# Gated FFN on one core: constant start-up matmuls in bfloat16 instead of fp8, and the weights of contraction blocks 2 and 3 in four DMAs instead of two

## Chip, cores, metric

One core of a Trainium2 chip. The metric is the device time of one execution in microseconds (us). The profile's span, from the first to the last instruction, is about 1.8 us shorter than the device time of the same execution.

## The reference

```python
def reference(x, w_gate, w_up, w_down):          # gelu with the tanh approximation
    return (_gelu(x @ w_gate) * (x @ w_up)) @ w_down
# x (32, 32, 1024), w_gate and w_up (1024, 3584), w_down (3584, 1024), all bfloat16
```

So 1024 rows, a contraction of 1024 (eight blocks of 128) for gate and up, and one of 3584 for the down projection.

## The kernel before

All instructions of an engine are emitted through one helper, which derives the semaphore waits; the profile therefore gives one line number (L98) to most of it (L163 is a second form of the matmul), and groups are told apart by tile names. `xT` is x transposed, with the contraction on the partitions, `wg` and `wu` are gate and up weights, `ps` is PSUM, `xn` is untransposed x for the first two blocks.

The head of the kernel is what the change touches:

```python
one = nc.const_aps.tensor(1.0, [P, 1], BF16).bitcast(mybir.dt.float8e4)[:, 0:1]
...                                              # identity matrix for the transposes
for n in [512] * 6 + [128] * 2:                  # constant matmuls, result never used
    pr.add("pe", "matmul", ps[:, 3, 0:n], one.broadcast_to([P, 2, P]), one.broadcast_to([P, 2, n]),
           start=True, stop=True, perf_mode=mybir.MatmulPerfMode.DoubleRow, w=[("ps", 3)])

NX = 2
... # x for blocks 0 and 1 (one DMA on each of two queues), then, block by block:
for k in range(NX):
    load_w("sp", "g", 0, k, k + 1)               # 128 KB each
    load_w("act", "u", 0, k, k + 1)
for k0, k1 in ((2, 3), (3, 4), (4, 5), (5, 6), (6, 8)):
    load_x(0, k0, k1)                            # transposing DMAs on SP's queue
load_w("act", "g", 0, 2, 4)                      # 256 KB each, on ACT's queue
load_w("act", "u", 0, 2, 4)
pr.add("act", "activation", warm[:, 0:1], const0, ACTF.Gelu_apprx_tanh)   # loads the table
... # PE transposes of xn for blocks 0 and 1, DVE copies to xT
... # then for k = 0..5: 4 gate matmuls and 4 up matmuls of 512 columns each;
    # after block 0 ACT issues g and u of blocks 4-5, after block 1 those of 6-7
```

In the rest (not shown) TensorE runs through the other weights and the down projection.

## Time and profile before

| | before |
|---|---|
| device time, first three runs | 300.06 us median (299.28 to 300.16) |
| span of the profiled run (299.36 us, not one of the timed runs) | 297.6 us |
| TensorE busy | 294.3 us (99%) |
| first real matmul | 4.76 us |
| first matmul of block 2 | 8.56 us |

First line of the profile page's part 1 (busy us, share of the span, instructions by engine), kernel before. PE are TensorE's matmuls, PEld its weight loads, which overlap them, DVE is VectorE, ACT ScalarE and POOL GpSimd:

```profile
PE 294.3 (99%) x1388; PEld 78.2 (26%) x808; DVE 42.7 (14%) x68; ACT 37.3 (13%) x67; POOL 0.7 (0%) x6
```

TensorE's timeline of the first 10 us, kernel before. The columns are start, duration of the merged group, engine, line, operation, tiles, form and count; in brackets the idle time that the profile shows before it and what ended it:

```profile
0.77 3.01 PE L98 MATMUL ps<-const-bfloat16-1.0 128*128 128x1024 fp8e4 x8 [0.77 <-PEq L310]
3.64 0.92 PE L98 MATMUL ps<-ident,xn 128*128 128x128 bf16 x8
4.76 1.02 PE L98 MATMUL ps<-xT,wg 128*128 128x512 bf16 x4 [0.20 <-DVE xT L98]
5.62 1.03 PE L98 MATMUL ps<-xT,wu 128*128 128x512 bf16 x4
6.49 1.03 PE L98 MATMUL ps<-xT,wg 128*128 128x512 bf16 x4
7.35 1.03 PE L98 MATMUL ps<-xT,wu 128*128 128x512 bf16 x4
8.56 1.02 PE L98 MATMUL ps<-xT,wg 128*128 128x512 bf16 x4 [0.19 <-DMA xT<-in_x_dram]
```

A group of four matmuls at full rate has its successor 0.863 us later (5.62 to 6.49), 0.216 us per matmul. Between 7.35 and 8.56 lie 1.21 us, so TensorE stood still for about 0.35 us; the bracket says 0.19 because the modelled end of a matmul lies behind the moment at which the next one could have started. A group at half rate is longer than 1.03 us: this is how the clock is read here, because the page's clock row shows full clock throughout, also where the spacing is twice as long.

The chain that ended last, kernel before, in order of time (start, us, what); `DMA xT` from 2.21 lasting 6.22 means issued at 2.21 and landed at 8.43:

```profile
2.21 6.22 DMA xT<-in_x_dram
8.43 0.14 issue
8.56 11.60 PE ps L98 x53
```

From 8.56 us on TensorE never waits. In this run the last wait is thus the one for x block 2.

### The profile page before, as it was taken

The numbers are of one execution on the slowest core, as the hardware profiler recorded it, in microseconds if no ns is written. First come the engines' busy times: TensorE is split into PE (matmuls) and PEld (weight loads), VectorE is DVE, ScalarE is ACT, GpSimd is POOL, SyncE is SP. The second block draws the span as 40 slices with busy tenths as digits, with TensorE's granted clock in tenths as the row PEclk, the third lists the DMA queues.
The fourth block names the chain that finished last, engine by engine and source line by source line (L and its number), as shares of the span: only waits on it lengthen the run. The fifth ranks groups of instructions, "written<-read, shape, count | busy, mean of one in ns | idle before, by whom it ended". The sixth has DMA issues, their size and how long they took to land.

```text
span 297.6 us, 2575 instructions
## 1 busy us (share of the span) xinstructions
PE 294.3 (99%) x1388; PEld 78.2 (26%) x808; DVE 42.7 (14%) x68; ACT 37.3 (13%) x67; POOL 0.7 (0%) x6
## 2 busy tenths in 40 slices
PE   8999999999999999999999999999999999999997
PEld 4444322222222222222222222222222222222244
DVE  1030311111221111111111122110000000000000
ACT  1030411111111111221111111110000000000010
POOL 0000000000000000000000000000000000000000
PEclk9999999999999999999999999999999999999999
DMA  7999743006708409321030040000101101011011
GB/s 207 252 241 353 226 134 134 9 0 189 234 2 270 154 2 330 94 76 65 0 139 4 0 141 0 0 2 0 35 0 35 37 0 35 0 37 35 0 35 35
DMA packets 28842, 26.37 MB, mean 89 GB/s; under 512 B 8352, under 2 KB 25248, under 8 KB 28832
## 3 DMA queue, kind: packets, MB, share of 16 engines
q1 hardware_dynamic: 26640, 24.25, 26.3%
q10 hardware_dynamic: 2192, 1.97, 2.2%
q8 instruction: 8, 0.13, 0.2%
q14 instruction: 2, 0.02, 0.0%
HBM read 22.28 MB, written 2.10 MB: 82 GB/s over the span
## 4 chain that ended last, share of the span: by engine, by line
PE 96%; DMA 2%; SPq 0%; issue 0%; ACT 0%
PE ps L98 54%; PE ps L163 42%; DMA xT<-in_x_dram 2%; SPq L98 0%; ACT xT L98 0%
## 5 line engine op out<-in xcount | busy, mean ns | idle before, releaser
L98 PE MATMUL ps<-xT,wg 128*128 128x512 bf16 x256 | 90.2, 379 | 0.4 <-DVE xT L98 0.2
L98 PE MATMUL ps<-xT,wu 128*128 128x512 bf16 x256 | 90.2, 379 | 0.0
L98 PE MATMUL ps<-wd,hT 128*128 128x512 bf16 (+2 forms) x280 | 86.6, 358 | 0.0
L163 PE MATMUL ps<-wd,hT 128*128 128x512 bf16 x196 | 74.3, 379 | 0.0
L163 PE MATMUL ps<-xT,wg 128*128 128x512 bf16 x192 | 72.8, 379 | 0.0
L163 PE MATMUL ps<-xT,wu 128*128 128x512 bf16 x192 | 72.8, 379 | 0.0
L98 DVE TENSOR_TENSOR hT<-g,ps 128x512 bf16<-128x512 f32 x56 | 36.4, 685 | 158.5 <-PE ps L98 158.5
L98 ACT ACTIVATE g<-ps 128x512 f32<-128x512 f32 x56 | 30.8, 595 | 160.4 <-PE ps L98 160.4
L98 PEld LDWEIGHTS ps<-wd,hT 128*128 128x128 bf16 x280 | 26.0, 98 | 71.3 <-issue 65.8
L98 PEld LDWEIGHTS ps<-xT,wu 128*128 128x128 bf16 x256 | 25.0, 98 | 71.7 <-issue 64.1
L98 PEld LDWEIGHTS ps<-xT,wg 128*128 128x128 bf16 x256 | 24.9, 98 | 72.0 <-issue 64.8
L98 DVE CAST xT<-ps 128x512 bf16<-128x512 f32 (+1 forms) x8 | 5.4, 680 | 89.6 <-ACT xT L98 79.8
L98 ACT ACTIVATE xT<-ps 128x512 bf16<-128x512 f32 (+1 forms) x9 | 5.0, 558 | 94.6 <-PE ps L98 94.6
L98 PE MATMUL ps<-const-bfloat16-1.0 128*128 128x1024 fp8e4 (+1 forms) x8 | 3.0, 558 | 0.8 <-PEq L310 0.8
L98 PEld LDWEIGHTS ps<-const-bfloat16-1.0 128*128 128x256 fp8e4 x8 | 1.7, 218 | 1.9 <-issue 1.9
L98 ACT ACT_TABLE_LOAD x1 | 1.3, 1283 | 3.4 <-issue 3.4
L98 DVE COPY xT<-ps 128x256 bf16<-128x256 bf16 x4 | 0.9, 286 | 4.1 <-PE ps L98 4.1
L98 PE MATMUL ps<-ident,xn 128*128 128x128 bf16 x8 | 0.9, 278 | 0.0
L98 PEld LDWEIGHTS ps<-ident,xn 128*128 128x128 bf16 x8 | 0.6, 124 | 0.2
L98 POOL TENSOR_SCALAR_AFFINE_SELECT ident<-ident 128x128 bf16<-128x128 bf16 x1 | 0.3, 292 | 0.2 <-POOL ident L98 0.2
L98 POOL MEMSET ident<- 128x128 bf16 x1 | 0.2, 204 | 0.3 <-POOLq L310 0.3
L98 ACT ACTIVATE warm<-const-float32-0.0 128x1 f32<-128x1 f32 x1 | 0.2, 202 | 0.0
(4 smaller groups left out, 0.4 us busy)
## 6 DMA issues: line engine op xcount, KB each, us to landing
wd<-in_w_down_dram SPq DMA_DIRECT2D x7, 1024.0 KB, 5.4
wg<-in_w_gate_dram SPq DMA_DIRECT2D x6, 1024.0 KB, 7.4
wu<-in_w_up_dram SPq DMA_DIRECT2D x6, 1024.0 KB, 9.7
out_dram<-xT SPq DMA_DIRECT2D x15, 128.0 KB, 1.7
wg<-in_w_gate_dram ACTq DMA_DIRECT2D x3, 256.0 KB, 4.5
wu<-in_w_up_dram ACTq DMA_DIRECT2D x3, 256.0 KB, 4.9
wg<-in_w_gate_dram SPq DMA_DIRECT2D x2, 128.0 KB, 3.2
wu<-in_w_up_dram ACTq DMA_DIRECT2D x2, 128.0 KB, 3.5
```

Of the source, the lines that this page charges most:

```text
L98: ins = name(eng, *args, **kw) if callable(name) else getattr(eng, name)(*args, **kw)
L163: return eng.add_instruction(mybir.InstMatmult(start_tensor_calc=start, stop_tensor_calc=stop, ldweights=False, name=nc.get_next_instructi ...
```

## The change

The likely intent: the constant matmuls keep TensorE occupied so that its clock is up when the real work begins, and are to do that in the number format of the real work; and each weight piece is to arrive in the order of its use, so that block 2 does not wait for weights of block 3.

```diff
-        one = nc.const_aps.tensor(1.0, [P, 1], BF16).bitcast(mybir.dt.float8e4)[:, 0:1]
+        one = nc.const_aps.tensor(1.0, [P, 512], BF16)
 ...
-            pr.add("pe", "matmul", ps[:, 3, 0:n], one.broadcast_to([P, 2, P]), one.broadcast_to([P, 2, n]), start=True, stop=True,
-                   perf_mode=mybir.MatmulPerfMode.DoubleRow, w=[("ps", 3)])
+            pr.add("pe", "matmul", ps[:, 3, 0:n], one[:, 0:P], one[:, 0:n], start=True, stop=True, w=[("ps", 3)])
 ...
-        load_w("act", "g", 0, 2, 4)
-        load_w("act", "u", 0, 2, 4)
+        for k in range(2, 4):
+            load_w("act", "g", 0, k, k + 1)
+            load_w("act", "u", 0, k, k + 1)
```

## The prediction

> **What bounds the kernel now.** TensorE, nearly alone. The busy-share table gives PE 294.3 of a 297.6 us span; the chain that ended last is 96% PE and 2% the DMA that transposes x. In the timeline 512-column matmuls start 0.216 us apart from 8.57 us to the tail without a hole. The work is 1344 of them, about 290 us (estimate from that spacing), so 7.7 us are left, and the change touches only the first 9 us. After its start TensorE waits twice: 0.2 us for the copy of the transposed x and 0.2 us for the DMA of x block 2 (waits view); from the instruction starts the true holes are about 0.2 us at 4.6 and 0.35 us at 8.2.
>
> **Constant matmuls.** Eight run before any data is there, from 0.77 to about 3.6 us. In the timeline the six long ones start 0.427 us apart, twice the later 0.215: half rate, and fp8 with two rows gains nothing. "TensorE: Matmul & The Clock Gate" of the Trainium skill (section "Back-to-back issue gap") gives N/1.2 ns for a cold bf16 matmul, 427 ns at 512. So bf16 should keep 0.427 us each; only the first weight load shrinks (0.18 to 0.1 us), and the block ends perhaps 0.03 us earlier. The transposes behind it wait for the DMAs of x (landed 3.60 and 3.85 us): no gain. Their purpose is to bring the clock up: full-rate spacing appears between 4.2 and 4.4 us, 3.5 us after the first constant matmul, and all real matmuls (from 4.77 us) run at full rate. bf16 keeps TensorE as densely occupied; I expect the same switch. The same page ("What's actually happening") says the window is free-running, so its moment may shift from run to run, worth at most 1.7 us (a 3.4 us window at half rate), for either kernel. The runs before (299.28 to 300.16) may already show this.
>
> **Weights in four pieces.** Same bytes. Two DMA issues of 0.46 and 0.58 us on ScalarE's queue become four, about 1 us more, which moves the activation table load (1.28 us, at 3.37) to about 4.3; the first gelu is at 16.1 us, so this is free. Landings before: g blocks 2-3 at 6.7 us, u at 8.3, x block 2 at 8.43. TensorE needs g and x of block 2 at 8.2 us, u at 9.4, block 3 at 10.3 and 11.2. The last to arrive is x, not a weight. Smaller pieces bring g block 2 to about 6.1 us and u block 2 to about 6.9; both are useless alone. All four pieces are queued before about 5.5 us, so they share the DMA engines with x blocks 2 and 3 much as before; I expect x block 2 at 8.4 +- 0.4 us. Later pieces have over 1.5 us of slack.
>
> **Sum.** Gain at most the 0.35 us hole, expected 0 to 0.1 us; loss under 0.5 us if the transposes come later. Predicted 299.9 us, 8 in 10 between 298.9 and 300.9. Faster by over 2% 0.01, within 2% 0.98, slower by over 2% 0.01.
>
> **What would show it right.** Constant matmuls still 0.427 us apart; real matmuls 0.215 us apart from the first; the wait at 8.3 us still ended by the DMA of x and of like length; PE's busy time the same within 2 us; the u weights of block 2 landing over 1 us earlier with no effect.
>
> **What would make it wrong.** bf16 ones not releasing the clock in time (real matmuls 0.43 us apart until about 7 us, +1 to 2 us), or doing so sooner in most runs (down to -1 us); the regrouped weight DMAs delaying x block 2, which each 0.1 us pays in full.

## The result

| | before | after |
|---|---|---|
| device time, six runs each, median | 300.08 us (299.28 to 300.16) | 299.37 us (298.96 to 299.97) |
| ratio after to before | | 0.9983, 95% interval 0.9968 to 0.9998 |
| span of the profiled run | 297.6 us | 297.9 us |

A ratio is the mean time of one kernel's fast runs over that of the other's of the same rounds, so not quite the ratio of the medians in the table. The timed runs say 0.17% less; the profiled run of after is longer than that of before. The two point in opposite directions, and both are small: this was the first sign that single runs of the same kernel differ by as much as the kernels do.

Part 1 of the page, kernel after:

```profile
PE 294.5 (99%) x1388; PEld 77.9 (26%) x808; DVE 42.7 (14%) x68; ACT 37.3 (13%) x67; POOL 0.7 (0%) x6
```

TensorE's timeline of the first 10 us, kernel after:

```profile
0.77 2.93 PE L98 MATMUL ps<-const-bfloat16-1.0 128*128 128x512 bf16 x8 [0.77 <-PEq L310]
3.50 1.06 PE L98 MATMUL ps<-ident,xn 128*128 128x128 bf16 x8
4.61 1.23 PE L98 MATMUL ps<-xT,wg 128*128 128x512 bf16 x4
5.68 1.03 PE L98 MATMUL ps<-xT,wu 128*128 128x512 bf16 x4
6.54 1.03 PE L98 MATMUL ps<-xT,wg 128*128 128x512 bf16 x4
7.41 1.03 PE L98 MATMUL ps<-xT,wu 128*128 128x512 bf16 x4
8.93 1.02 PE L98 MATMUL ps<-xT,wg 128*128 128x512 bf16 x4 [0.50 <-DMA xT<-in_x_dram]
```

The chain that ended last, kernel after:

```profile
2.21 6.58 DMA xT<-in_x_dram
8.79 0.14 issue
8.93 11.17 PE ps L98 x51
```

What to see. The constant block is 0.08 us shorter (3.01 to 2.93), which is what the first weight load got shorter: it covers 128 columns instead of 256 and takes 0.10 instead of 0.18 us. From the second on, the long ones start 0.427 us apart in both traces. Here x had landed early enough, so the transposes began at 3.50 and the real matmuls at 4.61 us instead of 4.76. But the first group of real matmuls takes 1.23 instead of 1.02 us: TensorE was still at half rate. That eats the 0.15 us. Then x block 2 lands at 8.79 instead of 8.43, and from 8.93 us everything follows 0.37 us later than before. The u weights of block 2 landed at 8.44 us here, later even than the double piece of before (8.28).

A bookkeeping makes the traces comparable. Call S the start of the first real matmul, H the time lost to half rate after S, and W the time for which TensorE stood still after S. H and W are read from the starts of consecutive matmuls: what goes beyond 0.216 us is H while the spacing is that of half rate, and W otherwise. (Gaps of exactly one matmul, without a wait, are matmuls missing from the record.) Then the span is 292.44 us + S + H + W in each of the eight traces of the two kernels below, to 0.05 us. All differences between these eight executions lie in these three terms.

### The profile page after: what moved, and what is told of

It reads as the page before. It is cut to its first block, busy times and chain, and to the rows that moved or that the text cites. A ratio compares the mean times of both kernels' runs of the same rounds, so it can differ in the third digit from the quotient of the medians.

```text
span 297.9 us, 2578 instructions
## 1 busy us (share of the span) xinstructions
PE 294.5 (99%) x1388; PEld 77.9 (26%) x808; DVE 42.7 (14%) x68; ACT 37.3 (13%) x67; POOL 0.7 (0%) x6
## 4 chain that ended last, share of the span: by engine, by line
PE 96%; DMA 2%; SPq 0%; issue 0%; ACT 0%
PE ps L98 54%; PE ps L163 42%; DMA xT<-in_x_dram 2%; SPq L98 0%; ACT xT L98 0%
## 5 line engine op out<-in xcount | busy, mean ns | idle before, releaser
L98 PE MATMUL ps<-const-bfloat16-1.0 128*128 128x512 bf16 (+1 forms) x8 | 2.9, 548 | 0.8 <-PEq L310 0.8
L98 PEld LDWEIGHTS ps<-const-bfloat16-1.0 128*128 128x128 bf16 x8 | 1.0, 140 | 2.4 <-issue 2.4
```

What stands on the lines that cost most here:

```text
L98: ins = name(eng, *args, **kw) if callable(name) else getattr(eng, name)(*args, **kw)
```

## Experiments

Twelve kernels ran. Unless stated, the profiled run is one of the timed ones.

### Same kernels again, and each half of the change alone

`c1_before_again` and `c2_after_again` are the two kernels unchanged. `e1_bf16_only` takes the first half of the change, `e2_split_only` the second:

```diff
 # e1_bf16_only, against before
-        one = nc.const_aps.tensor(1.0, [P, 1], BF16).bitcast(mybir.dt.float8e4)[:, 0:1]
+        one = nc.const_aps.tensor(1.0, [P, 512], BF16)
 ...  (and the matmul call as in the change)
 # e2_split_only, against before
-        load_w("act", "g", 0, 2, 4)
-        load_w("act", "u", 0, 2, 4)
+        for k in range(2, 4):
+            load_w("act", "g", 0, k, k + 1)
+            load_w("act", "u", 0, k, k + 1)
```

> The kernel before, unchanged, as a control. Theory A (neither part matters; the time is when x block 2 lands): ratio 1.000 within 0.15%, and the profile's first matmul of block 2 at 8.4 to 9.0 us. Theory B (the fp8 constant matmuls release the clock late in most runs, and the traced run of before was a lucky one): real matmuls of block 0 start 0.43 us apart until some moment after 5 us, and the runs cluster near 300.1 rather than 299.3 us.

> The kernel after, unchanged. Theory A: ratio to before within 0.998 to 1.001, not clear of 1. Theory B or C: 0.9975 to 0.999 again, clear of 1 (0.3 to 0.7 us less).

> Only the constant matmuls become bf16; weights of blocks 2 and 3 stay in two pieces. Theory A: ratio 0.999 to 1.001. Theory B (the clock): all of the gain, ratio near 0.998. Theory C (the gain is the order of the weight pieces): 1.000. In all: constant matmuls 0.427 us apart, the block ending about 0.08 us earlier as in the profile after.

> Only the weights of blocks 2 and 3 come in four pieces; constant matmuls stay fp8 in pairs of rows. Theory A: ratio 0.999 to 1.001. Theory B: 1.000. Theory C: near 0.998, with x block 2 landing earlier than in the control. Fourth possibility: slower by up to 0.4 us, as the profile after has x block 2 at 8.80 against 8.43 us.

| run, six runs each | median us | ratio to before | 95% interval | span of the profile |
|---|---|---|---|---|
| c1_before_again | 299.39 | 0.9991 | 0.9975 to 1.0007 | 297.3 |
| c2_after_again | 299.88 | 1.0005 | 0.9981 to 1.0029 | 298.9 |
| e1_bf16_only | 299.64 | 1.0006 | 0.9982 to 1.0029 | 297.3 |
| e2_split_only | 300.02 | 1.0007 | 0.9986 to 1.0028 | 297.7 |

(Theories A to E are those of the expectations printed with the runs.) Neither half gains. The 0.17% of the first comparison did not come back in c2, and the copy of before is itself 0.09% below before. Theories B (the clock) and C (the order of the pieces) had expected about 0.998 for one of the halves; both stood at 1.000 within 0.3%. The intervals reach down to 0.9982 and 0.9986, so a gain of 0.1 to 0.2% is not excluded by these runs; it is only not seen.

The traces showed more than the times. In c2 the wait had moved. TensorE's waits, c2 (engine, line, tile, what it waited for, us in total, times, longest):

```profile
PE ps L98 <- DMA wu<-in_w_up_dram: 1.2, 1, 1.2
```

The chain that ended last, c2, in its middle:

```profile
7.49 6.73 DMA wu<-in_w_up_dram
14.22 0.05 issue
14.26 5.79 PE ps L98 x26
```

The DMA that was issued at 7.49 us is that of the u weights of blocks 4 and 5, which the change does not touch. In the first trace of before it had landed at 11.43 us, here only at 14.22, and TensorE waited for it. In the three traces with two pieces so far (before, c1, e1), x blocks 6 and 7 had landed by 12.5 us, in the three with four pieces (after, c2, e2) between 14.2 and 15.2. That suggested theory D: more pieces slow the DMA engines while the transposes run.

### No constant matmuls; the weights later; another order; eight pieces

```diff
 # e3_no_const, against before
-        for n in [512] * 6 + [128] * 2:
+        for n in []:
 # e4_late_two, against before: the table load ahead of the two weight DMAs
+        pr.add("act", "activation", warm[:, 0:1], const0, ACTF.Gelu_apprx_tanh)
         load_w("act", "g", 0, 2, 4)
         load_w("act", "u", 0, 2, 4)
-        pr.add("act", "activation", warm[:, 0:1], const0, ACTF.Gelu_apprx_tanh)
 # e5_split_gguu, against before
-        load_w("act", "g", 0, 2, 4)
-        load_w("act", "u", 0, 2, 4)
+        for kind in "gu":
+            for k in range(2, 4):
+                load_w("act", kind, 0, k, k + 1)
 # e6_eight, against before: pieces of 64 partitions, in the order of use; table load moved
 # behind the loads of blocks 4 to 7
+        for k in range(2, 4):
+            for kind in "gu":
+                ...
+                for p0 in (0, 64):
+                    pr.add("act", "dma_start", dst[0][p0:p0 + 64, k:k + 1, :], src[p0:p0 + 64, k:k + 1, 0:GW * P], ...)
```

> The kernel before without its constant matmuls. If they bring the clock up in time (all theories of the clock): the first real matmuls start 0.43 us apart until 7 to 10 us instead of 0.215, 1 to 2 us are lost there, and part is given back because the waits for x block 2 shrink: ratio 1.001 to 1.006. If the clock came up by itself in any case: ratio 1.000 and full rate by 5.7 us at the latest.

> The kernel before with the activation table load ahead of the weights of blocks 2 and 3, which so are issued about 1.5 us later, still in two pieces. If the later issue of the last pieces is what made x blocks 3 to 7 and weights of blocks 4 and 5 land late in the three profiles with four pieces (x blocks 6 and 7 at 14.2 to 15.2 us against 12.3 to 12.5, u of blocks 4 and 5 at 12.8 to 14.2 against 11.4 to 11.7): they land as late here. If it is the number of pieces: they land as in before, at most 0.5 us later. Time: 0.999 to 1.003.

> Four pieces in the order g2, g3, u2, u3 instead of g2, u2, g3, u3. If the number of pieces counts: x blocks 6 and 7 land at 14 to 15 us and u of blocks 4 and 5 near 13 us as in the profiles with four pieces. If the order counts: near before, 12.3 to 12.5 and 11.4 to 11.7 us. Time: 0.998 to 1.003 in both, not to be told from 1.

> The weights of blocks 2 and 3 in eight pieces of 64 partitions, in the order of use, rows of 1 KB as before; the activation table load moved behind the loads of blocks 4 to 7 so that it does not hold them up. If more pieces slow the DMA engines while the transposes run: x blocks 6 and 7 land at 15 us or later, u of blocks 4 and 5 later than 13 us and after TensorE wants them (12.9 us), waits of TensorE of 0.5 to 3 us in the profile, ratio 1.002 to 1.008. If the number of pieces has no part in it: landings as in before or as with four pieces, ratio 1.000.

| run, four runs each | median us | ratio to before | 95% interval |
|---|---|---|---|
| e3_no_const | 300.72 | 1.0041 | 1.0011 to 1.0071 |
| e4_late_two | 299.48 | 1.0002 | 0.9976 to 1.0029 |
| e5_split_gguu | 299.73 | 1.0010 | 0.9984 to 1.0035 |
| e6_eight | 300.53 | 1.0039 | 1.0010 to 1.0068 |

**e3** tells what the constant matmuls are for. TensorE's timeline without them:

```profile
3.34 1.07 PE L98 MATMUL ps<-ident,xn 128*128 128x128 bf16 x8 [3.34 <-DMA xn<-in_x_dram]
4.46 1.86 PE L98 MATMUL ps<-xT,wg 128*128 128x512 bf16 x4
6.12 1.26 PE L98 MATMUL ps<-xT,wu 128*128 128x512 bf16 x4
7.21 1.03 PE L98 MATMUL ps<-xT,wg 128*128 128x512 bf16 x4
```

The real matmuls begin earlier (4.46 us) but five intervals run at half rate, until about 6.6 us. Those intervals exceed 0.216 us by 0.16 us once and by 0.21 us four times, so H is 1.0 us, and the kernel is 0.41% slower, as expected (half rate ended a little before the 7 us that the expectation named). So the constant matmuls are worth about 0.4% here (0.1 to 0.7% by the interval). The trace, of e3's fastest run, accounts for a part of that: 1.0 us of H, and 0.21 us of waiting for u of blocks 4 and 5, less the 0.3 us by which S is earlier. With them, in either number format, H lay between 0 and 0.5 us in every trace.

**e4** did not do what it was built for: the table load runs from 2.27 to 3.55 us, but the two weight DMAs were issued at 2.33 and 2.77 us all the same, hardly later than in before. It is therefore no test of the later issue. But it served as one more trace with two pieces, and there x blocks 6 and 7 landed at 14.7 us, late. In e3, also with two pieces, they landed at 14.6. Theory D was in doubt.

**e5**, with four pieces in the other order, had them at 14.5 us, and u of blocks 4 and 5 at 12.4. This fits D and shows no part of the order, in one trace.

**e6** is slower by 0.39%. TensorE's waits:

```profile
PE ps L98 <- DMA wu<-in_w_up_dram: 0.5, 2, 0.3
PE ps L98 <- DMA wg<-in_w_gate_dram: 0.3, 1, 0.3
```

W is 1.6 us in four gaps, each ended by the landing of a weight piece (the view has three of them; the fourth, 0.26 us, is hidden by the modelled end of the matmul before it). The eight issues took about 0.62 us each, so the last one began at 6.97 us, and g of blocks 4 and 5 was issued at 7.63 us, although block 0 would have allowed it at about 6.7 us, as in before. The x blocks 6 and 7 landed at 13.3 us, earlier than D wanted. This points to the pieces being issued one behind the other as the cost, and not to transposes that are held up; no run varied the issue times alone, so it is not shown.

### Four more traces of the two kernels

The last four runs went to theory D against theory E, a stall by chance. `r1_before` and `r3_before` are before, `r2_after` and `r4_after` are after, unchanged.

> The kernel before again, for its trace. Theory D (more pieces slow the DMA engines): 215 to 250 GB/s from 4.7 to 9.5 us and x blocks 6 and 7 landed by 12.6 us, as in three of the five traces with two pieces. Theory E (a stall of the engines at about 5 us, long or short by chance, whatever the pieces): may as well be 160 to 205 GB/s and landed after 14 us. Time: 299.7 us on average (mean of the 30 runs of before so far 299.67), ratio 0.998 to 1.002.

> The kernel after again. Theory D: 160 to 205 GB/s from 4.7 to 9.5 us, x blocks 6 and 7 landed after 14 us, as in all four traces with four pieces. Theory E: at times 215 to 250 GB/s and landed by 12.6 us. Time: ratio 0.998 to 1.002 (mean of the 12 runs so far 299.68 us).

> As the other copy of before. The two copies of before together: under D both fast in the window, under E either. The clock comes up anywhere between 4.2 and 7.6 us in both kernels.

> As the other copy of after: under D both slow in the window, under E either. All copies of this call within 0.2% of the runs of before on average; the two copies of one kernel differ from each other as much as before from after.

| run, six runs each | median us | ratio to before | 95% interval |
|---|---|---|---|
| r1_before | 299.42 | 0.9978 | 0.9954 to 1.0002 |
| r2_after | 299.62 | 0.9992 | 0.9970 to 1.0013 |
| r3_before | 299.59 | 0.9993 | 0.9969 to 1.0018 |
| r4_after | 299.41 | 0.9985 | 0.9959 to 1.0010 |

The work of all engines from 4.7 to 9.5 us, r1_before. The columns are the stretch, its length, busy us and instructions of PE, PEld, DVE, ACT and POOL, the clock, the mean busy share of the DMA engines (over 1 where packets overlap) and GB/s:

```profile
4.70:9.50 4.80, 3.79 (x16) 1.38 (x16) 0.29 (x2) 0.30 (x2) 0.00 (x0) 1.00 1.17 167
```

The same stretch in r4_after:

```profile
4.70:9.50 4.80, 4.75 (x22) 2.13 (x22) 0.36 (x2) 1.49 (x2) 0.00 (x0) 1.00 1.22 211
```

The kernel with two pieces moved 167 GB/s, the lowest of the eight traces of the two kernels, and the one with four 211. D had before at 215 or more and after at 205 or less; copies of before (167 and 196) and one copy of after (211) fell outside. As a claim about the throughput, D has fallen. The whole picture, in which landing times are those of the DMA completion in the trace:

| trace | g, block 2 | x, block 2 | u, block 2 | u, blocks 4-5 | x, blocks 6-7 | GB/s | S | H | W | span |
|---|---|---|---|---|---|---|---|---|---|---|
| before, first | 6.72 | 8.43 | 8.28 | 11.43 | 12.26 | 248 | 4.76 | 0 | 0.35 | 297.6 |
| c1 (before) | 7.71 | 7.69 | 8.58 | 11.66 | 12.48 | 219 | 4.71 | 0.13 | 0 | 297.3 |
| r1 (before) | 9.47 | 8.44 | 10.58 | 13.34 | 16.47 | 167 | 4.71 | 0 | 1.59 | 298.8 |
| r3 (before) | 7.71 | 7.87 | 9.22 | 12.67 | 12.91 | 196 | 4.71 | 0.45 | 0 | 297.6 |
| after, first | 7.93 | 8.79 | 8.44 | 12.78 | 14.82 | 169 | 4.61 | 0.21 | 0.66 | 297.9 |
| c2 (after) | 7.10 | 7.58 | 8.06 | 14.22 | 15.24 | 200 | 4.75 | 0.41 | 1.34 | 298.9 |
| r2 (after) | 7.64 | 8.45 | 8.40 | 13.88 | 15.20 | 171 | 4.61 | 0.46 | 1.10 | 298.6 |
| r4 (after) | 6.66 | 7.80 | 7.75 | 11.81 | 13.59 | 211 | 4.78 | 0.20 | 0 | 297.4 |

In r1_before the wait is the one that the change was made against: TensorE's waits,

```profile
PE ps L98 <- DMA wg<-in_w_gate_dram: 1.0, 1, 1.0
```

and its timeline at that place:

```profile
9.51 1.04 PE L98 MATMUL ps<-xT,wg 128*128 128x512 bf16 x4 [0.98 <-DMA wg<-in_w_gate_dram]
10.63 0.82 PE L98 MATMUL ps<-xT,wu 128*128 128x512 bf16 x3
```

The double piece of g lands at 9.47, a microsecond after x block 2. In none of the four traces of after, nor in e2 and e5, did TensorE wait for a weight of block 2 or 3. In two of the four traces of after it waited instead for u of blocks 4 and 5. TensorE's waits in r2_after, the second of these:

```profile
PE ps L98 <- DMA wu<-in_w_up_dram: 0.9, 1, 0.9
```

And in r4_after nothing was waited for after the start. The chain that ended last there runs through TensorE alone:

```profile
4.78 7.48 PE ps L98 x33
12.26 0.05 issue
12.32 7.72 PE ps L98 x35
```

The times, taken together: the mean over all 53 runs of before in the four sets of rounds (its copies among them) is 299.74 us, that over all 24 runs of after is 299.66 us. The difference of 0.08 us has a standard error of 0.15 us, worked out from the scatter of single runs (0.54 and 0.63 us). Without the first comparison, whose interval lay just below 1, the means are 299.71 us for before (47 runs) and 299.74 us for after (18 runs): the sign is the other one. The three copies of before have ratios to before of 0.9991, 0.9978 and 0.9993, mean 0.9987; the four sets of after have 0.9983, 1.0005, 0.9992 and 0.9985, mean 0.9991. A copy of the same program "gained" as much as the change.

## Why the prediction was right

**How much of it was luck.** The prediction put 299.9 us into the middle of a range 2 us wide. The runs of the two kernels, copies included, went from 298.8 to 301.4 us, and 73 of the 77 lie in that range; the number would have been met with a wrong account of the head, and in part it was. Of the signs that the prediction named, the constant matmuls' spacing and TensorE's busy time held in all traces. The real matmuls were not at full rate from the first in six of the eight traces, and the wait for x block 2 was there in only two of the four traces of after, with 0.66 and 0.07 us.

**What bounds the kernel: right.** TensorE is busy for 294.3 and 294.5 us, and the span is 292.44 us plus three small terms of the head in all eight traces. Only S, H and W can move the time.

**Constant matmuls keep 0.427 us: right.** 0.427 us in both formats. "TensorE: Matmul & The Clock Gate" of the Trainium skill ("Back-to-back issue gap") gives N/1.2 ns for a cold bf16 matmul of N columns, so 427 ns for 512, and the traces agree. The gain of 0.03 us was too low, the block is 0.08 us shorter. "No gain", because x comes later, holds in c2 and r4 (S 4.75 and 4.78), but not where x came early: after and r2 had S = 4.61. That is 0.1 to 0.15 us in two traces of four.

**The clock: right that both formats bring it up before 5.8 us, wrong that every real matmul is at full rate.** That was read from one trace, whose execution happened to have the clock up early. H was 0 to 0.45 us in the other traces of before. The page's account ("What's actually happening") that the window is free-running was the reason for expecting scatter, and scatter there is; it reached 0.5 us. H was 0.20 to 0.46 us in the four traces of after, and 0 in two of before. On the average of these four and four traces, after has 0.04 us less of S and 0.17 us more of H.

The packed traces (`trace.npz`, array `0/clock`) hold what the views do not print: the moment at which full clock was granted. It agrees with H: 4.27 us in the first trace of before, 5.00 in c1 and 5.65 in r3; 5.07 in the first trace of after, 5.60 in c2, 5.57 in r2 and 5.22 in r4 (r1 has no such record). In all eleven traces with a record full clock lasted 293.546 us, and ended 2.3 us (c2) to 4.1 us (e3) after the last matmul: the end kept its distance from the beginning, not from the kernel's own end. Counting the other kernels that have constant matmuls, the first real matmul was at full rate in four of eight traces with fp8 (before, r1, e5, e6) and in none of five with bf16 (after, c2, r2, r4, e1). That is a hint that bf16 lets the clock up later; from so few traces it is not shown.

**Smaller pieces: no effect on the time, as predicted; wrong in the landing times.** The prediction had g of block 2 at 6.1 and u at 6.9 us. They landed at 6.7 to 7.9 and at 7.8 to 8.5 us, against 6.7 to 9.5 and 8.3 to 10.6 for the double pieces. On average u came 1.0 us earlier (0.5 us without r1), where the prediction had 1.4 us, and from a later level. x block 2 landed at 7.6 to 8.8 us in both kernels; the prediction's 8.4 +- 0.4 held in one half of the traces, the rest were earlier. "The last to arrive is x, not a weight" was again read from the one trace: r1_before shows the double piece of g last, and 1.1 us lost.

**What was missing: the blocks behind.** The prediction looked at blocks 2 and 3 and gave them 1.5 us of slack (block 3 had about 0.8 us in the first trace of after: g landed at 9.82 and was used at 10.65). It did not look at blocks 4 and 5. Their u weights are used at about 12.9 us and landed at 11.4 to 13.3 us in before, 11.8 to 14.2 in after. Two traces of after lost 1.0 and 1.3 us there.

So the time stayed the same while S, H and W each moved, from one execution to the next and in copies of the same kernel as much as between the two: the places where TensorE can be kept waiting are several and close to one another. That the change takes one wait away and brings another in is not shown. The wait for a weight of block 2 was seen in one of the seven traces with two pieces (r1) and in none of the six with four. But the wait for u of blocks 4 and 5 does not belong to four pieces alone: e3, with two, has it too (u landed at 13.42 us and TensorE stood still for 0.21 us), and in r1 that u landed at 13.34 us, when TensorE was already late. Over 24 and 53 runs no difference is seen beyond the error of 0.15 us.

What stays open: the four-piece kernels have x blocks 6 and 7 at 13.6 to 15.2 us in all six traces (e2 and e5 among them), the two-piece ones at 12.3 to 12.9 in four traces (e1 among them) and at 14.6 to 16.5 in three (e3, e4, r1). So four pieces may make the late landing likelier, and that could be how the wait at blocks 4 and 5 comes about; that cause was argued, not shown. Why the DMA engines stall was not settled either. In every trace the longest packet in flight near 5.0 us, just after the first packets of the transposing DMAs (4.1 to 4.8 us), took 0.4 to 1.7 us, where the median packet of a weight took 0.046 us; packets of 0.3 us and more come again between 7 and 9.4 us. "DMA: Bandwidth & Descriptors" of the Trainium skill ("Issuing engines are not separate DMA queues") says that DMAs of all issuing engines share the same 16 DMA engines and interleave; the traces fit that, since weights on one queue and transposes on another are late together, but it does not say why a stall is short or long.

No version of these experiments beats both kernels: the best span of a profile, 297.3 us, was reached by before itself (c1) and by e1, when H and W happened to be small.

## What to carry to other kernels

When a kernel is at 99% on one engine, write its span as a constant plus the few terms that can still move, and read each from several traces: one trace shows one throw of the dice, and here the first one misled about the clock and about which DMA comes last. Before a gain of 0.2% is believed, run an unchanged copy under a new name; here it showed a "gain" as large. And when a load is cut up or moved, check the slack of the loads queued behind it, not only that of the pieces themselves.

## What the Trainium skill lacked or had wrong

- "TensorE: Matmul & The Clock Gate" ("Weight-path perf modes") gives DoubleRow a gain of about 1.44 over bf16 when warm. It has nothing for half rate: here both formats start a matmul of 512 output columns every 0.427 us, and the DoubleRow one reads twice the elements for them (128x1024 against 128x512 in the timelines). Its "LDWEIGHTS +72%", measured warm, was here 218 against 140 ns on average at half rate, 56% more.
- The same page ("What's actually happening") asks for a busy window of about 3.4 us before full rate. In e3 full rate came about 3.2 us after the first transpose and 2.1 us after the first real matmul; it also says in "Part 4" that full rate does not engage in transpose mode. So either the transposes counted as busy time here, or 2.1 us of it were enough. And in e5 the PE transposes themselves went from 0.107 us apart to 0.056 us apart at about 3.9 us, so they do run at full rate (the profile lists them as MATMUL and does not say in which mode they ran).
- No page has the stall of single packets at about 5 us, when DMA transposes begin beside ordinary loads: 0.4 to 1.7 us for the longest against a median of 0.046 us. In one and the same kernel the throughput from 4.7 to 9.5 us was 248 GB/s where the longest such packet took 0.5 us (before) and 167 GB/s where it took 1.7 us (r1); that the one causes the other is not shown.
- "DMA: Bandwidth & Descriptors" calls the time to initiate a DMA usually small relative to the DMA. Each is small here too: in e6 a piece of 64 KB took about 0.62 us to issue and landed 4.7 to 5.3 us after its issue began. But the issues of one engine follow one another, and the eighth began only at 6.97 us (e6 was 0.39% slower).
- No page says whether a table load holds up the DMA issues behind it on ScalarE. It did not: issued at 2.33 and 2.77 us while the load ran from 2.27 to 3.55 us (e4).
